# Chunk 2's first accumulator in two PSUM tiles, and two pieces of start-up work moved, in a TensorE-bound convolution and MLP kernel

## The chip, the cores and the metric

One core of a Trainium2 chip runs the whole program. The metric is the device time of one execution in microseconds. Times are quoted as medians. A profiled execution has a *span*, which starts at its first instruction; all moments below are microseconds from there. The *granted clock* is the share of its full clock that TensorE had, as the profile records it; over the whole span it is 1.0 or 0.999 in every run.

## The reference, cut to what matters

```python
def _attn_ref(x, weight):                    # x (8, 4096, 192), weight (8 heads, 7 taps)
    w = softmax(weight, axis=-1)             # (cut: written out in the original)
    x_pad = np.concatenate([zeros(B, 6, D), x], axis=1)
    ...                                      # each output row: 7 rows of x, weighted per head
def _moe_ref(x, w_in, w_out):                # w_in (192, 2048), w_out (2048, 192)
    h = x @ w_in
    g = np.maximum(0.01 * h, h)
    return g @ w_out                         # (32768, 192) float32
```

A causal convolution of 7 taps with one set of weights per head, then a first product, a leaky ReLU and a second product.

## The kernel before

The 192 channels are three *chunks* of 64. Two sequences lie on partitions 0 to 63 and 64 to 127. TensorE's matmuls write into *tiles* (buffers) of a memory called PSUM; such a tile, an *accumulator*, has to be copied out by ScalarE or VectorE, which the prediction calls evacuation. The first eight *groups* have 256 columns, the others 512. VectorE convolves nearly all groups ahead of need; for group 0 (all chunks) and group 1 (chunks 0 and 2) TensorE does it, with diagonal matrices of tap weights, because there is nothing else to run yet. Chunk 2 is convolved *crosswise*: its halves change partitions, so its matmuls use the two quarters of the TensorE array that chunks 0 and 1 leave free: where two chunks are convolved together, four matmuls start within 0.02 us (6.60 to 6.61 in the trace of before) and the next four 0.11 later. Its accumulator has to be copied out in two halves, each back to its own partitions.

```python
    def pe_conv_jobs(grp, c, parts=(0, 1), cross=False):
        blk, t0, T = grp
        acc = psum_o.tile([128, ST], FP32, name="acc", tag="po")     # one PSUM tile (pool of 4)
        ...                                                          # cut: matmuls diag * xt into acc
        def evac(*scale):
            ...
            if not cross:
                scale[0](y, acc[:, :T], rsum[:, c, :])
                return
            for e in range(2):
                ps = slice(e * CH, (e + 1) * CH)
                frm = slice((1 - e) * CH, (2 - e) * CH)
                scale[e](y[ps], acc[frm, :T], rsum[frm, c, :])
        return jobs, evac
    ...
    run(pe_0[:K])
    run(pe_0[K:], pe_2[:K])
    evac_0(act_scale)                                     # ScalarE
    run(pe_1[:K], pe_2[K:])
    run(pe_1[K:])
    evac_1(act_scale)                                     # ScalarE
    evac_2(act_scale, nc.vector.tensor_scalar_mul)        # half on ScalarE, half on VectorE
    transpose_first(1)                                    # TensorE, input of the next 256 rows
```

The first product takes one *product* `u` at a time: 12 matmuls into one of two accumulators `ph`, which one ScalarE activation then empties. In the main loop, group 0 looks so:

```python
            for u in range(2 * j, 2 * j + 2):
                mm1(grp, u, 128 if i <= NSW else CH)      # product u, then its activation
                ...
                if i == 0 and u in CUTS:                  # behind u = 1, 3, 4
                    cut = slice(*CUTS[u])
                    run(pe_0[cut], pe_2[cut])             # convolution of group 1
                if i == 0 and u == 5:
                    evac_0(act_scale)
                    evac_2(nc.vector.tensor_scalar_mul, nc.vector.tensor_scalar_mul)
                if i == 0 and u == 6:
                    transpose_first(2)
```

From group 1 on, *slots* (small groups of matmuls) of the second product (`po`, later `acc2`) fill TensorE between the first products.

Of the kernel before, what the change touches and what calls it, by code (L numbers as in the profile page):

```python
# [10 lines left out]
FP32 = mybir.dt.float32  # L11
# [4 lines left out]
def kernel(  # L16
# [8 lines left out]
    nc = tc.nc  # L25
# [10 lines left out]
    CH = 64  # L36
    NCH = D // CH
    ST = 512
# [6 lines left out]
    NHALF = 4  # L45
    RUN = 4
    NPEC = 3
    CUTS = {1: (0, 5), 3: (5, 10), 4: (10, 14)}
    GB = 32
    NR = D // (2 * GB)  # L50
# [9 lines left out]
    psum_o = ctx.enter_context(tc.tile_pool(name="po", bufs=4, space=bass.MemoryType.PSUM))  # L60
# [6 lines left out]
    groups = [(b, h * HT, HT) for b in range(NHALF) for h in range(2)]  # L67
# [100 lines left out]
    def evac_first(q, *copies):  # L168
        dst = xt[0][:, :, HALO + q * HT : HALO + (q + 1) * HT]
        dst = dst.rearrange("p c (s k) -> p s c k", s=HS)  # L170
        for s, t in enumerate(ptr.pop(q)):
            copies[s](out=dst[:, s], in_=t)  # L172
# [37 lines left out]
                    )  # L210
        return jobs

    def pe_conv_jobs(grp, c, parts=(0, 1), cross=False):



        blk, t0, T = grp
        acc = psum_o.tile([128, ST], FP32, name="acc", tag="po")
        jobs = []
        for p in parts:  # L220
            for k in range(K):
                a = BASE + k + blk * ST + t0
                both = []
                for e in range(2):
                    ps = slice(e * CH, (e + 1) * CH)
                    to = slice((e ^ cross) * CH, ((e ^ cross) + 1) * CH)
                    both.append(
                        lambda k=k, p=p, a=a, ps=ps, to=to: nc.tensor.matmul(  # L228
                            out=acc[to, :T], lhsT=diag[c][ps, p, k, :],
                            rhs=xt[0][ps, c, a : a + T],  # L230
                            start=(k == 0 and p == parts[0]),
                            stop=(k == K - 1 and p == parts[1]),
                        )
                    )
                jobs.append(both)

        def evac(*scale):
            if blk not in yt:
                yt[blk] = yt_pool.tile([128, NCH, ST], BF16, name="yt")
            y = yt[blk][:, c, t0 : t0 + T]  # L240
            if not cross:
                scale[0](y, acc[:, :T], rsum[:, c, :])
                return
            for e in range(2):
                ps = slice(e * CH, (e + 1) * CH)
                frm = slice((1 - e) * CH, (2 - e) * CH)
                scale[e](y[ps], acc[frm, :T], rsum[frm, c, :])  # L247

        return jobs, evac

    def run(*lists):
        for slots in zip_longest(*lists, fillvalue=()):
            for both in slots:
                for job in both:
                    job()
# [12 lines left out]
    for sign, off in ((1, 0), (-1, GRP - 1)):  # L268
        nc.gpsimd.affine_select(
            out=sel, in_=sel, compare_op=mybir.AluOpType.is_ge, fill=0.0,  # L270
# [16 lines left out]
    def spread_down(n):  # L287
        nc.vector.tensor_copy(out=w_in[n][0:CH, 1, :], in_=w_in[n][CH:128, 0, :])

    def spread_up(n):  # L290
        nc.vector.tensor_copy(out=w_in[n][CH:128, 1:3, :], in_=w_in[n][0:CH, 0:3:2, :])

    def w_in_of(f, e, c, m0, m1):
        n, f = divmod(f, NFC // NPW)
        slot = c if c == 2 else c ^ e
        a = f // RUN * RUN * 128 + f % RUN
        return w_in[n][
            e * CH : (e + 1) * CH, slot, a + m0 * RUN : a - f % RUN + m1 * RUN : RUN
        ]
# [6 lines left out]
    for rows in (0, 128):  # L306
# [6 lines left out]
        out=w_out.rearrange("p (c i) d -> p c i d", i=RUN),  # L313
# [8 lines left out]
    def warm(n, cols=HT):  # L322
# [10 lines left out]
        out=nmax, in_=w9[:, 0:K], axis=mybir.AxisListType.X,  # L333
# [3 lines left out]
        out=w9[:, 0:K], in_=w9[:, 0:K], func=mybir.ActivationFunctionType.Exp,  # L337
# [37 lines left out]

    diag = [const_pool.tile([128, 2, K, CH], BF16, name=f"diag{c}") for c in range(NPEC)]

# [21 lines left out]
    for p in range(2):  # L399
        diag_wide(2, p, K)  # L400
    spread_down(0)
    rsum = const_pool.tile([128, NCH, 1], FP32)
# [3 lines left out]
        out=rsum, in0=wml[:, :, K:], scalar=1e-9, in1=whm[:, :, 0, K:],  # L406
# [7 lines left out]
    def act_scale(out, in_, scale):  # L414
        nc.scalar.activation(  # L415
            out=out, in_=in_, func=mybir.ActivationFunctionType.Copy, scale=scale
        )

    pe_0, evac_0 = pe_conv_jobs(groups[0], 0)
    pe_2, evac_2 = pe_conv_jobs(groups[0], 2, cross=True)  # L420
    pe_1, evac_1 = pe_conv_jobs(groups[0], 1, (1, 0))
    run(pe_0[:K])
    run(pe_0[K:], pe_2[:K])
    evac_0(act_scale)
    run(pe_1[:K], pe_2[K:])
    run(pe_1[K:])
    evac_1(act_scale)
    evac_2(act_scale, nc.vector.tensor_scalar_mul)
    transpose_first(1)
    evac_first(1, nc.vector.tensor_copy, nc.vector.tensor_copy)  # L430
    wk = const_pool.tile([128, NCH, K], FP32, name="wk")
# [4 lines left out]
    g, po, acc2, osb, seal = {}, {}, {}, {}, None  # L436
# [8 lines left out]
    def mm1(grp, u, M):  # L445
        blk, t0, T = grp
        y = yt[blk]
        nf = ST // T
        ph = psum_h.tile([128, 2, ST], FP32, name="ph", tag="ph")
        for i in range(nf):  # L450
            f = nf * u + i
            for c in range(NCH):
                for e in range(2):
                    ps = slice(e * CH, (e + 1) * CH)
                    for m in range(0, 128, M):
                        nc.tensor.matmul(  # L456
                            out=ph[m : m + M, e, i * T : (i + 1) * T],
                            lhsT=w_in_of(f, e, c, m, m + M),
                            rhs=y[ps, c, t0 : t0 + T],
                            start=(c == 0),  # L460
                            stop=(c == NCH - 1),
                        )
        act = nc.scalar.activation(  # L463
            out=g[blk][:, nf * u : nf * (u + 1), :, t0 : t0 + T],
            in_=ph.rearrange("p e (i t) -> p i e t", i=nf),
            func=mybir.ActivationFunctionType.Prelu, alpha=0.01,
        )
        return act
# [143 lines left out]
    for i, grp in enumerate(groups):  # L612
        blk, t0, T = grp
        steps = T // 64
        if t0 == 0:
            g[blk] = g_pool.tile([128, NFC, 2, ST], BF16, name="g", tag="g")
        quota = plan.get(i, [16] * 4 if T == HT else [5, 5, 6, 5, 5, 6, 8, 8])

        if i == 0:
            ahead = []  # L620
        else:
            ahead = conv_jobs(groups[i + 1]) if i + 1 < len(groups) else []
        per = -(-len(ahead) // steps)
        for j in range(steps):
            for u in range(2 * j, 2 * j + 2):
                mm1(grp, u, 128 if i <= NSW else CH)
                if i == 0 and u == 0:
                    conv_1 = conv_jobs(groups[1], (1,))
                    for job in conv_1[:3]:
                        job()  # L630
                    spread_down(1)
                    spread_up(1)
                    for job in conv_1[3:]:
                        job()
                    pe_0, evac_0 = pe_conv_jobs(groups[1], 0)
                    pe_2, evac_2 = pe_conv_jobs(groups[1], 2, cross=True)
                if i == 0 and u in CUTS:
                    cut = slice(*CUTS[u])
                    run(pe_0[cut], pe_2[cut])
                if i == 0 and u == 5:  # L640
                    evac_0(act_scale)
                    evac_2(nc.vector.tensor_scalar_mul, nc.vector.tensor_scalar_mul)
                if i == 0 and u == 6:
                    transpose_first(2)
            jobs = ahead[per * j : per * (j + 1)]
            if T == ST:


                jobs = ahead[len(ahead) * j // steps : len(ahead) * (j + 1) // steps]
                for job in jobs:  # L650
                    job()
                jobs = []
            for _ in range(quota[j]):
                if i <= NSW:
                    mm2_row_slot(slot)
                else:
                    mm2_slot(slot)
                slot += 1
            if i == 0 and j == 3:
                evac_first(2, nc.vector.tensor_copy, nc.vector.tensor_copy)  # L660
            if i == 2 and j == 1:
                transpose_x(2)
            for job in jobs:
                job()
            if i == 0 and j == 3:
                transpose_half(3)

            last_half = t0 + T == ST
            if i == NSW and j == steps - 1:
                evac_o(LAST - 1)  # L670
                slot = NSW * NR * NFC
            if j == steps // 4 and last_half:
                load_x(blk + 3)
            if j == steps // 2 and last_half and blk > 0:
                transpose_x(blk + 2)
# [35 lines left out]
```

## Time and profile before

| | before |
|---|---|
| median of the first three runs | 686.46 us (685.19 to 686.69) |
| span of the profiled run | 683.4 us |
| TensorE busy | 677.7 us (99%) |
| first activation starts | 11.06 |
| first matmul of a second product starts | 20.79 |

The prediction shows the engine totals, the chain and the wait of VectorE. The view below gives the busy time of each engine in stretches of the span (stretch, its length, then the engines with their instruction counts, the granted clock, DMA share and GB/s), for the kernel before:

```profile
0.00:20.79 20.79, 18.50 (x312) 13.35 (x313) 15.44 (x46) 16.66 (x34) 16.91 (x31) 1.00 1.09 143
20.79:60.00 39.21, 39.21 (x840) 39.21 (x837) 34.13 (x92) 33.22 (x46) 16.04 (x23) 1.00 0.85 92
60.00:640.00 580.00, 579.75 (x10760) 382.82 (x10760) 421.42 (x689) 452.30 (x521) 113.03 (x152) 1.00 0.58 76
640.00:683.40 43.40, 40.25 (x680) 29.00 (x668) 11.55 (x20) 22.39 (x26) 0.00 (x0) 1.00 0.23 56
```

Behind the length of each stretch stand TensorE's busy time and, in brackets, its instructions. Once second products have begun, TensorE is busy in 39.21 of 39.21 and 579.75 of 580.00 us. In the first 20.79 us it is idle for 2.29; a change of the order at the start can help only there. The 3.15 us idle in the last stretch lie behind the last matmul (over at 680.26), where the last copy and output transfers are left.

### The profile page before, as it was taken

The numbers are of one execution on the slowest core, as the hardware profiler recorded it, in microseconds if no ns is written. First come the engines' busy times: TensorE is split into PE (matmuls) and PEld (weight loads), VectorE is DVE, ScalarE is ACT, GpSimd is POOL, SyncE is SP. The second block draws the span as 40 slices with busy tenths as digits, with TensorE's granted clock in tenths as the row PEclk, the third lists the DMA queues.
The fourth block names the chain that finished last, engine by engine and source line by source line (L and its number), as shares of the span: only waits on it lengthen the run. The fifth ranks groups of instructions, "written<-read, shape, count | busy, mean of one in ns | idle before, by whom it ended". The sixth has DMA issues, their size and how long they took to land.

```text
span 683.4 us, 27404 instructions
## 1 busy us (share of the span) xinstructions
PE 677.7 (99%) x12575; PEld 464.4 (68%) x12575; DVE 482.5 (71%) x844; ACT 524.6 (77%) x624; POOL 146.0 (21%) x204
## 2 busy tenths in 40 slices
PE   9999999999999999999999999999999999999998
PEld 6999986666666666666666666666666666666667
DVE  7979758667687667687667786676876676876612
ACT  7888998777777777777778777777777778777781
POOL 7722222222102222112221022221022220000000
PEclk9999999999999999999999999999999999999999
DMA  9975668557466566565564665574665664321123
GB/s 155 93 101 76 84 79 98 61 60 94 78 89 81 60 73 92 80 90 74 56 84 79 87 92 68 56 93 79 89 82 64 69 91 75 72 55 34 34 49 93
DMA packets 211763, 53.29 MB, mean 78 GB/s; under 512 B 205120, under 2 KB 211264, under 8 KB 211648
## 3 DMA queue, kind: packets, MB, share of 16 engines
q0 software_dynamic: 98736, 13.97, 29.9%
q1 hardware_dynamic: 112896, 37.57, 27.8%
q8 instruction: 98, 1.61, 1.0%
q14 instruction: 17, 0.14, 0.1%
q10 hardware_dynamic: 16, 0.00, 0.0%
HBM read 28.31 MB, written 25.17 MB: 78 GB/s over the span
## 4 chain that ended last, share of the span: by engine, by line
PE 97%; ACT 2%; DVE 0%; issue 0%; ACTq 0%
PE ph L456 48%; PE acc L545 41%; PE po L482 7%; ACT g L463 2%; PE acc L228 1%; ACT yt L415 0%; ACT L330 0%; ACTq L259 0%; ACT diag L387 0%; DVE yt L247 0%; ACT xt L172 0%; DVE o_sb L593 0%; DVE x_half L137 0%; ACT w L336 0%; ACT junk L330 0%
## 5 line engine op out<-in xcount | busy, mean ns | idle before, releaser
L463 ACT ACTIVATE g<-ph 128x1024 bf16<-128x1024 f32 x512 | 496.2, 1021 | 137.0 <-PE ph L456 136.6
L206 DVE SCALAR_TENSOR_TENSOR yt<-xt,wk,yt 128x512 bf16<-128x512 bf16 (+1 forms) x618 | 383.5, 702 | 0.2
L456 PE MATMUL ph<-yt,w_in 64*64 64x512 bf16 (+2 forms) x6048 | 378.4, 363 | 1.3 <-ACT g L463 0.6
L545 PE MATMUL acc<-g,w_out 64*64 64x512 bf16 x5184 | 316.5, 376 | 0.0
L456 PEld LDWEIGHTS <-w_in 64*64 64x64 bf16 (+1 forms) x6048 | 238.0, 129 | 99.1 <-issue 3.8
L545 PEld LDWEIGHTS <-w_out 64*64 64x64 bf16 x5184 | 166.7, 118 | 110.2
L82 POOL DMA_DIRECT2D x_bf<-in_x_dram x180 | 134.2, 770 | 416.2 <-DMA xt<-x_bf 309.9
L567 DVE STREAM_TRANSPOSE o_t<-acc 128x512 f32<-128x512 f32 x81 | 68.1, 885 | 169.5 <-PE acc L545 169.5
L482 PE MATMUL po<-w_out,g 64*128 64x192 bf16 (+1 forms) x1152 | 60.1, 243 | 0.0
L482 PEld LDWEIGHTS <-g 64*128 64x128 bf16 (+1 forms) x1152 | 55.6, 94 | 1.6 <-issue 0.4
L200 DVE TENSOR_SCALAR yt<-xt,wk 128x512 bf16<-128x512 bf16 (+1 forms) x103 | 28.8, 338 | 16.6 <-DMA xt<-x_bf 16.4
L555 ACT COPY junk<-junk 128x1 f32<-128x1 f32 x54 | 10.3, 192 | 3.9
L593 ACT COPY o_sb<-po 128x192 f32<-128x192 f32 x32 | 10.1, 320 | 1.3
L593 DVE COPY o_sb<-po 128x192 f32<-128x192 f32 x8 | 2.8, 357 | 6.8 <-PE po L482 3.9
L228 PE MATMUL acc<-xt,diag 64*64 64x256 bf16 x140 | 5.5, 272 | 0.3 <-ACT xt L172 0.3
L228 PEld LDWEIGHTS <-diag 64*64 64x64 bf16 x140 | 4.3, 106 | 1.4 <-issue 0.6
L324 PE MATMUL warm<-const-bfloat16-1.0 128*128 128x512 bf16 (+2 forms) x9 | 3.7, 521 | 0.8 <-PEq L695 0.8
L131 POOL DMA_DIRECT2D x_half<-in_x_dram x6 | 4.3, 757 | 0.0
L387 ACT ACTIVATE diag<-ident,whm 128x64 bf16<-128x64 bf16 x14 | 3.5, 335 | 0.2 <-DVE whm L373 0.2
L127 POOL DMA_DIRECT2D x_rows<-in_x_dram x4 | 2.9, 740 | 0.0
L330 ACT ACT_TABLE_LOAD x1 | 1.3, 1283 | 1.4 <-PEq L695 1.4
L324 PEld LDWEIGHTS <-const-bfloat16-1.0 128*128 128x128 bf16 x9 | 1.0, 122 | 2.0 <-issue 1.9
(44 smaller groups left out, 23.4 us busy)
## 6 DMA issues: line engine op xcount, KB each, us to landing
out_dram<-o_t SPq DMA_DIRECT2D x108, 192.0 KB, 4.6
x_bf<-in_x_dram POOLq DMA_DIRECT2D x180, 64.0 KB, 3.1
out_dram<-o_sb SPq DMA_DIRECT2D x16, 192.0 KB, 2.8
xt<-x_bf SPq DMA_TRANSPOSE x90, 3.7
w_out<-in_moe_w_out_dram POOLq DMA_DIRECT2D x1, 768.0 KB, 8.7
out_dram<-o_sb SPq DMA_DIRECT2D x8, 96.0 KB, 1.9
w_in<-in_moe_w_in_dram POOLq DMA_DIRECT2D x2, 256.0 KB, 4.7
x_nat<-in_x_dram SPq DMA_DIRECT2D x2, 192.0 KB, 2.5
```

Of the source, the lines that this page charges most:

```text
L82: nc.gpsimd.dma_start(out=t[:, c, :, e, :], in_=src[2 * rp + e, :, :, c * CH : (c + 1) * CH],)
L200: lambda s=src, d=dst, c=c: nc.vector.tensor_scalar_mul(d, s, wk[:, c, 0:1])
L206: lambda s=src, d=dst, c=c, k=k: nc.vector.scalar_tensor_tensor(out=d, in0=s, scalar=wk[:, c, k : k + 1], in1=d, op0=mybir.AluOpType.mult, ...
L228: lambda k=k, p=p, a=a, ps=ps, to=to: nc.tensor.matmul(out=acc[to, :T], lhsT=diag[c][ps, p, k, :], rhs=xt[0][ps, c, a : a + T], start=(k = ...
L324: nc.tensor.matmul(out=wa[:, 0, 0:cols], lhsT=ones[:, 0:128], rhs=ones[:, 0:cols], start=True, stop=True,)
L456: nc.tensor.matmul(out=ph[m : m + M, e, i * T : (i + 1) * T], lhsT=w_in_of(f, e, c, m, m + M), rhs=y[ps, c, t0 : t0 + T], start=(c == 0), ...
L463: act = nc.scalar.activation(out=g[blk][:, nf * u : nf * (u + 1), :, t0 : t0 + T], in_=ph.rearrange("p e (i t) -> p i e t", i=nf), func=my ...
L482: return nc.tensor.matmul(out=po[m], lhsT=g[b][ps, fc, e, s * 128 : (s + 1) * 128], rhs=w_out[ps, fc, :], start=start, stop=stop,)
L545: ins = nc.tensor.matmul(out=acc2[gi, r][e * CH : (e + 1) * CH, 0:T], lhsT=w_out_of(ps, fc, r), rhs=g[b][ps, fc, e, t0 : t0 + T], start=fi ...
L555: seal = nc.scalar.copy(out=junk, in_=junk)
L567: nc.vector.transpose(out=osb[gi, 0][:, 0 : T // GB, :, r], in_=acc2.pop((gi, r))[:, 0:T].rearrange("p (j k) -> p j k", k=GB),)
L593: ins = copy(out=o_sb[:, n % 2, :], in_=po.pop(n))
```

## The change

Its intent: let ScalarE and VectorE copy the two halves of chunk 2 at the same time; copy chunk 2 before chunk 1, since it is complete earlier; let the first product use the chunks in that order; and move a copy and a block of transposes of the first group to places thought idle.

```diff
+    FIRST = (0, 2, 1)
...
-    def pe_conv_jobs(grp, c, parts=(0, 1), cross=False):
+    def pe_conv_jobs(grp, c, parts=(0, 1), cross=False, apart=False):
-        acc = psum_o.tile([128, ST], FP32, name="acc", tag="po")
+        accs = [
+            psum_o.tile([128, ST], FP32, name=f"acc{i}", tag="po")
+            for i in range(2 if apart else 1)
+        ]
...                                    (matmuls and copies use accs[e * apart])
-    pe_2, evac_2 = pe_conv_jobs(groups[0], 2, cross=True)
+    pe_2, evac_2 = pe_conv_jobs(groups[0], 2, cross=True, apart=True)
...
+    evac_2(act_scale, nc.vector.tensor_scalar_mul)
     evac_1(act_scale)
-    evac_2(act_scale, nc.vector.tensor_scalar_mul)
...                                    (mm1)
+        chunks = range(NCH) if blk or t0 else FIRST
...
                 if i == 0 and u == 5:
-                    evac_0(act_scale)
+                    evac_0(nc.vector.tensor_scalar_mul)
                     evac_2(nc.vector.tensor_scalar_mul, nc.vector.tensor_scalar_mul)
-                if i == 0 and u == 6:
+                if i == 0 and u == 7:
                     transpose_first(2)
```

As in the prediction: **A** is everything up to `FIRST`, **B** the copy of chunk 0 of group 1 on VectorE, **C** the transposes behind the eighth product (`u == 7`) instead of the seventh.

More of the change, by code (lines that the diff above doesn't have):

```diff
@@ L227, in pe_conv_jobs @@
                     both.append(
-                        lambda k=k, p=p, a=a, ps=ps, to=to: nc.tensor.matmul(
+                        lambda k=k, p=p, a=a, ps=ps, to=to, acc=accs[e * apart]: nc.tensor.matmul(
                             out=acc[to, :T], lhsT=diag[c][ps, p, k, :],
@@ L241, in evac @@
             if not cross:
-                scale[0](y, acc[:, :T], rsum[:, c, :])
+                scale[0](y, accs[0][:, :T], rsum[:, c, :])
                 return
@@ L246, in evac @@
                 frm = slice((1 - e) * CH, (2 - e) * CH)
-                scale[e](y[ps], acc[frm, :T], rsum[frm, c, :])
+                scale[e](y[ps], accs[e * apart][frm, :T], rsum[frm, c, :])
         return jobs, evac
@@ L449, in mm1 @@
         ph = psum_h.tile([128, 2, ST], FP32, name="ph", tag="ph")
-        for i in range(nf):
+        chunks = range(NCH) if blk or t0 else FIRST
+        for n in range(nf * NCH):
+            i, c = n // NCH, chunks[n % NCH]
             f = nf * u + i
-            for c in range(NCH):
-                for e in range(2):
-                    ps = slice(e * CH, (e + 1) * CH)
-                    for m in range(0, 128, M):
-                        nc.tensor.matmul(
-                            out=ph[m : m + M, e, i * T : (i + 1) * T],
-                            lhsT=w_in_of(f, e, c, m, m + M),
-                            rhs=y[ps, c, t0 : t0 + T],
-                            start=(c == 0),
-                            stop=(c == NCH - 1),
-                        )
+            for e in range(2):
+                ps = slice(e * CH, (e + 1) * CH)
+                for m in range(0, 128, M):
+                    nc.tensor.matmul(
+                        out=ph[m : m + M, e, i * T : (i + 1) * T],
+                        lhsT=w_in_of(f, e, c, m, m + M),
+                        rhs=y[ps, c, t0 : t0 + T],
+                        start=(c == chunks[0]),
+                        stop=(c == chunks[-1]),
+                    )
         act = nc.scalar.activation(
```

## The prediction

> **What bounds the kernel now.** I read the page first: engine totals, the chain that ended last, the costliest groups. Then the chain in order of time for the first 45 us, because the diff touches only the work of the first two groups of 256 columns. Last, ScalarE and VectorE in order of time there.
>
> From the page (engine totals; the chain by engine; one group):
>
> ```profile
> PE 677.7 (99%) x12575; PEld 464.4 (68%) x12575; DVE 482.5 (71%) x844; ACT 524.6 (77%) x624; POOL 146.0 (21%) x204
> ...
> PE 97%; ACT 2%; DVE 0%; issue 0%; ACTq 0%
> ...
> L456 PE MATMUL ph<-yt,w_in 64*64 64x512 bf16 (+2 forms) x6048 | 378.4, 363 | 1.3 <-ACT g L463 0.6
> ```
>
> TensorE sets the time. It is busy in 677.7 of 683.4 us; all waits of the first-product matmuls come to 1.3 us. The other engines can only matter where TensorE waits for them, and 97% of the chain never leaves TensorE. The 3% elsewhere is the start. The chain there (start, duration, what):
>
> ```profile
> 5.45 3.42 PE acc L228 x84
> 8.88 0.02 issue
> 8.90 0.47 ACT yt L415
> 9.37 0.03 issue
> 9.40 0.48 ACT yt L415
> 9.88 0.02 issue
> 9.90 0.49 DVE yt L247
> 10.39 0.04 issue
> 10.43 1.25 PE ph L456 x19
> ...
> 16.73 1.02 ACT g L463
> 17.76 0.03 issue
> 17.78 0.47 ACT yt L415
> 18.26 1.84 ACT g L463 x2
> 20.09 0.04 issue
> 20.14 0.85 PE ph L456 x12
> 20.98 1.32 PE po L482 x32
> ```
>
> Two pieces are not TensorE's. From 8.90 to 10.39 three evacuations run one after another: chunk 1 (ScalarE), the first half of chunk 2 (ScalarE), its second half (VectorE). From 16.73 to 20.09 four ScalarE operations follow each other, one of them chunk 0's evacuation for the second group. From 20.14 the chain alternates two TensorE pieces of about 1.31 us without a break: there the time is TensorE's own.
>
> VectorE over the first piece (start, duration, engine, line, operation, idle before it and its releaser):
>
> ```profile
> 8.05 0.80 DVE L291 COPY w_in<-w_in 64x2048 bf16<-64x2048 bf16 x1
> 9.90 0.48 DVE L247 TENSOR_SCALAR yt<-acc,rsum 64x256 bf16<-64x256 f32 x1 [1.04 <-ACT yt L415]
> ```
>
> VectorE stood idle for 1.04 us until ScalarE was done, although the halves lie on different partitions of the accumulator. That is the wait the change is after.
>
> **What the Trainium skill says.** (1) "PSUM — Partial Sum Buffer", section "PSUM bank collisions raise a hardware error": two engines must be kept apart by bank and quadrant of 32 partitions, reads against reads included; guarding by bank alone is the simple version. The trace agrees with the simple version: halves of 64 partitions in one bank were still put in sequence, at 1.04 us. Two tiles mean two banks, so that order can go. (2) "ScalarE: Activation LUTs", section "What ACT_TABLE_LOAD costs": 186 ns + 0.833 ns per column, about 93 ns more for a pointer scale. For 256 columns I estimate 492 ns; the trace has 0.47, used below. It counts columns, not partitions: the half tile costs as much as the whole (0.48 against 0.47). (3) "TensorEngine Tiling (Array Packing)", section "PSUM Bottleneck": evacuate with both ScalarE and VectorE. The third part of the change does that in the second group. (4) "VectorE: DVE Perf Modes", "Side-by-side: where the cycles go": one result per cycle in the basic mode plus some 158 cycles of fill and start. I estimate (256+158)/0.96 = 431 ns for an evacuation from PSUM; the trace has 0.48, used below.
>
> **Part by part.** No matmul, copy or byte is added or removed.
>
> *A, the first group.* Chunk 2's accumulator lies in two tiles, it is copied before chunk 1, and the first product takes the chunks as 0, 2, 1. Chunk 2's convolution is complete seven column slots before chunk 1's. Slots start 0.11 us apart and the last at 8.59, so chunk 2's last starts at about 7.82 and is done (0.27 us) by 8.09. ScalarE started chunk 0's copy at 8.18; its copies start 0.50 apart (8.90, 9.40). So chunk 2's first half starts at 8.68 and chunk 1 at 9.18, done at 9.65. VectorE ends its weight copy at 8.85 and has the other half done at 8.87 + 0.48 = 9.35. TensorE is still in its transposes until 9.24; it does chunk 0, then chunk 2 at about 9.4, and waits for chunk 1 until 9.65 + 0.04 = 9.69. Before, the last wait ended at 10.43. As many pairs of matmuls come behind that wait as before. Gain: 10.43 − 9.69 = **0.74 us**.
>
> I take this gain as passed on whole to 17.8: from 10.43 on the chain is TensorE's own order of products and convolution slots, and ScalarE's activations follow those. VectorE also gets its copies of the second quarter done earlier (9.37 instead of 10.41), so it won't become the bound.
>
> *B, chunk 0's copy of the second group goes from ScalarE to VectorE.* In times of before: activations that follow each other directly start 0.97 apart (two in 1.94). With the copy between, the starts were 16.73 and 18.16, 1.43 apart. Removing it frees 0.46. But the matmuls of the eighth product, the last of group 0, start only when the sixth activation has freed its accumulator (16.73 + 1.02 = 17.75, started at 17.81), and B does not move that. From the first matmul of a product to its activation takes 0.89 (15.84 to 16.73). So the eighth activation can start at 17.81 + 0.89 = 18.70 instead of 18.16 + 0.97 = 19.13: 0.43 is left. VectorE pays 0.48, at a place where it delivers 4 us before need (its convolution for group 2 ended at 26.2; that group begins at about 30).
>
> *C, transposes of the third quarter behind the eighth product instead of before it.* Before, they filled a hole: 17.28 to 17.81, while TensorE waited for an accumulator anyway. Now they fall behind: last pair at about 18.36, a change of tile form of 0.20, 0.53 of transposes, next product at 19.09, and the second one after it at 19.09 + 0.66 = 19.75. ScalarE would allow 20.14 − 0.43 = 19.71. So C costs 0.04 of B, and B with C gives 20.14 − 19.75 = **0.39 us**. VectorE's copy of those transposes comes some 0.4 us later relative to TensorE; within the 4 us.
>
> Sum: 0.74 + 0.39 = **1.13 us**, 0.16% of the time. Behind 20.14 nothing stops TensorE, so I expect the whole of it at the end: span 683.4 − 1.1 = 682.3.
>
> **Rivals.** *R1: the order of the two reads stays*, because the halves also write one tile of the convolved input. For it: the trace cannot say which of the two tiles made VectorE wait. Against it: at 4.95 and 5.00 ScalarE and VectorE copy at once from two accumulators into disjoint columns of one tile. Even then VectorE would run 9.17 to 9.65, together with chunk 1, so it costs at most some hundredths: reordering alone brings A. *R2: pool turn-over.* One tile more in a pool of four: the second half takes a transpose tile copied out by 5.4, before it is needed; the next transposes take chunk 0's, copied out at 8.63, and start at 8.79. A wait here would show as TensorE waiting for ScalarE near 8.8, and cost 0.1 or so. *R3: ScalarE's own pace.* If the eight activations limited group 0 all the way, A would be lost. They wait 0.17, 0.28 and 0.32 for TensorE between 13 and 17, so they do not. *R4: given back later*, by transposed input arriving by DMA: VectorE waits 16.4 us for it in all, TensorE never. At 45.3 the convolution of group 4 ended, needed at about 51: 1.1 us earlier leaves over 4. If a hidden wait did return, the time would stay at 686.4. *R5: C blocks more* (the transposes wait for their tile or for rows): 0.3 us lost, 685.6.
>
> **Range and chances.** The median before is 686.46, but its three runs span 685.19 to 686.69 (mean 686.11) and the profiled one took 685.16: the noise is larger than the effect. 686.46 − 1.13 = 685.33; from the mean it would be 684.98. I take 685.2. Two tenths of a microsecond for R5 and the working, with noise of some 0.7 for a median of three, give 684.2 to 686.2. Two per cent is 13.7 us; nothing here reaches a tenth of it in either direction, so within 2% is nearly sure, 0.99.
>
> **What would show it right or wrong.** Right: VectorE's half of chunk 2 starts at 8.9 with no wait for ScalarE; a single wait of TensorE remains in the first product, for ScalarE, ending at about 9.7; the first activation starts near 10.3 instead of 11.06; no ScalarE copy stands between activations near 17; second products begin near 19.7 instead of 20.8 and last matmuls end 1.1 us earlier. A gain at 10.3 without one at 20 puts the fault in B or C; a gain at 20 without one at the end would be R4. A time over 686.5 or under 683.8 from fast runs would make the prediction wrong.

## The result and the profile after

| | before | changed |
|---|---|---|
| median, 6 runs each | 686.58 us (685.19 to 687.35) | 684.88 us (684.26 to 686.19) |
| span of the profiled run | 683.4 | 682.4 |
| first activation starts | 11.06 | 10.41 |
| first matmul of a second product | 20.79 | 19.77 |

The ratio is 0.9981, with a 95% interval from 0.9965 to 0.9997: the same within 2%. A ratio here is the mean time of one kernel's fast runs over that of the other's of the same rounds, so it is not quite the ratio of the medians. The predicted 685.2 lies 0.3 above the measured median, inside the range of 684.2 to 686.2.

Engine totals of the changed kernel, from its page:

```profile
PE 677.2 (99%) x12575; PEld 467.1 (68%) x12575; DVE 481.4 (71%) x845; ACT 524.2 (77%) x623; POOL 145.9 (21%) x204
```

One instruction has passed from ScalarE to VectorE (624 and 844 before), and no matmul was added. The chain in order of time, changed kernel (start, duration, what):

```profile
5.52 3.40 PE acc L232 x84
8.92 0.46 PE ptr L162 x12
9.38 0.34 PE ph L461 x4
9.72 0.02 issue
9.74 1.28 PE ph L461 x20
...
16.08 1.03 ACT g L468
17.11 0.04 issue
17.16 0.85 PE ph L461 x12
18.01 0.46 PE ptr L162 x12
18.46 1.50 PE ph L461 x24
19.97 1.32 PE po L487 x32
```

The three evacuations between 8.90 and 10.39 have left the chain; TensorE now goes from the convolution through its transposes straight into the first product. Near 17 one activation is left in it instead of a row of four ScalarE operations. The transposes (`ptr`) stand in it in both places. VectorE in order of time, changed kernel:

```profile
8.12 0.78 DVE L295 COPY w_in<-w_in 64x2048 bf16<-64x2048 bf16 x1
8.82 0.46 DVE L251 TENSOR_SCALAR yt<-acc,rsum 64x256 bf16<-64x256 f32 x1
```

Its half starts straight behind its weight copy, with no wait; before, it stood idle for 1.04 us. By stretches, changed kernel:

```profile
0.00:19.77 19.77, 17.98 (x312) 13.14 (x313) 13.84 (x43) 16.11 (x33) 15.06 (x29) 1.00 1.04 141
19.77:60.00 40.23, 40.23 (x864) 40.23 (x860) 36.19 (x98) 34.44 (x47) 18.97 (x26) 1.00 1.06 97
60.00:640.00 580.00, 579.74 (x10758) 385.33 (x10757) 419.88 (x687) 451.86 (x521) 111.87 (x151) 1.00 0.57 76
```

The same 312 matmuls now take 19.77 us, with 1.79 of TensorE idle time instead of 2.29. Most of the rest of the gain is in its busy time, though the work is the same: 1.83 before and 1.54 now from the start of the transposes to the first activation (31 matmuls each), 3.42 and 3.23 from the sixth activation to the first second product (61 each). The ends of matmuls in a profile are modelled, and a matmul in front of a wait counts as busy up to that end: this view counts part of the waiting as busy. From there on TensorE is as full as before. The first second product comes 1.02 earlier and the span is 1.02 shorter: nothing was given back.

### The profile page after: what moved, and what is told of

Read it like the earlier page. It is cut to its first block, busy times and chain, and to the rows that moved or that the text cites. A ratio compares the mean times of both kernels' runs of the same rounds, so it can differ in the third digit from the quotient of the medians.

```text
span 682.4 us, 27404 instructions
## 1 busy us (share of the span) xinstructions
PE 677.2 (99%) x12575; PEld 467.1 (68%) x12575; DVE 481.4 (71%) x845; ACT 524.2 (77%) x623; POOL 145.9 (21%) x204
## 4 chain that ended last, share of the span: by engine, by line
PE 97%; ACT 2%; DVE 0%; issue 0%; ACTq 0%
PE ph L461 48%; PE acc L550 41%; PE po L487 7%; ACT g L468 1%; PE acc L232 1%; PE ptr L162 0%; ACT L334 0%; ACTq L263 0%; ACT diag L391 0%; ACT xt L173 0%; DVE o_sb L598 0%; DVE x_half L138 0%; ACT w L340 0%; ACT junk L334 0%; DVE w9p L348 0%
## 5 line engine op out<-in xcount | busy, mean ns | idle before, releaser
L550 PEld LDWEIGHTS <-w_out 64*64 64x64 bf16 x5184 | 168.4, 119 | 108.4
L598 ACT COPY o_sb<-po 128x192 f32<-128x192 f32 x32 | 10.1, 320 | 1.3
L173 DVE COPY xt<-ptr 128x384 bf16<-128x384 bf16 x5 | 1.6, 352 | 1.8 <-PE ptr L162 1.7
```

What stands on the lines that cost most here:

```text
L550: ins = nc.tensor.matmul(out=acc2[gi, r][e * CH : (e + 1) * CH, 0:T], lhsT=w_out_of(ps, fc, r), rhs=g[b][ps, fc, e, t0 : t0 + T], start=fi ...
L598: ins = copy(out=o_sb[:, n % 2, :], in_=po.pop(n))
```

## The experiments

Twelve runs were made. Of e1 to e9, eight fell into a start that differs from that of the two profiles above: the convolution of group 0 runs at about half speed for part of its time. Absolute moments are then not comparable, so I cut each profile at four landmarks: T, the start of the transposes of the second quarter, which follow the convolution; the first activation; the sixth activation; the first matmul of a second product. The clock column is the moment from which the trace's own record of the granted clock (in the packed trace; no view prints it) shows full speed. The matmuls agree with it: in e9 the steps of the convolution start 0.21 apart until 10.1 and 0.11 apart from there on.

| kernel | full clock from | T | T to 1st activation | 1st to 6th | 6th to 2nd product | 2nd product to end |
|---|---|---|---|---|---|---|
| before | 4.2 | 8.79 | 2.27 | 5.67 | 4.06 | 662.65 |
| changed | 3.5 | 8.85 | 1.56 | 5.67 | 3.69 | 662.65 |
| e1 A alone | 9.1 | 10.62 | 1.34 | 5.67 | 3.93 | 662.65 |
| e2 A in one tile | 3.9 | 8.77* | 1.79* | 5.67 | 3.93 | 662.65 |
| e3 tiles, old order | 8.2 | 10.14 | 1.80 | 5.67 | 4.06 | 662.65 |
| e4 B and C alone | 8.3 | 10.22 | 2.28 | 5.67 | 3.69 | 662.65 |
| e5 without C | 9.0 | 10.56 | 1.35 | 5.67 | 3.69 | 662.66 |
| e6 copy twice | 10.1 | 11.10 | 1.82 | 5.67 | 3.69 | 662.66 |
| e7 second product early | 10.1 | 11.10 | 1.56 | 5.67 | 3.69 | 662.66 |
| e8 slots in the gap | 10.1 | 11.07 | 1.35 | 5.67 | 3.68** | 663.69 |
| e9 changed again | 10.1 | 11.07 | 1.35 | 5.68 | 3.69 | 662.65 |
| e10 more warm-up | 6.7 | 9.40 | 1.35 | 5.67 | 3.69 | 662.63 |
| e11 warm-up, old kernel | 6.6 | 9.33 | 2.28 | 5.68 | 4.05 | 662.64 |
| e12 more warm-up again | 6.1 | 9.09 | 1.62 | 5.67 | 3.69 | 662.65 |

\* one transpose at 8.77, the other eleven at 9.22, when their input rows had landed; 1.34 from there.

\*\* up to the second product behind group 0, at 21.77; the four slots that e8 moved start at 17.88.

The last column is the same to 0.03 us in all but e8. So the end follows from the first second product, and the parts can be judged by the columns between. Each run up to e8 is a single execution with a profile, so its own time is not used against others.

### e1: part A alone

```diff
-                    evac_0(nc.vector.tensor_scalar_mul)
+                    evac_0(act_scale)
-                if i == 0 and u == 7:
+                if i == 0 and u == 6:
```

> Part A alone; B and C undone. Theory (A and B+C are independent and each passes whole to the end): the first activation starts at about 10.4 as in the changed kernel (before: 11.06), the first second product at 20.79 - 0.65 = 20.1 (changed: 19.77), the span is near 683.4 - 0.65 = 682.75. Rival (ScalarE's pace limits the first group, so A is worth something only together with B): first activation 10.4, but the first second product at 20.6 or later and the span at 683.3.

Measured: 685.95 us, span 684.2, with the late clock, so neither expected moment could be met as written. By segments: T to the first activation is 1.34, against 2.28 in e4, which has the old first group and the late clock too. A brings 0.94 there, and it passes on whole: the next segment is unchanged and the last but one is even 0.13 shorter than before (3.93 against 4.06). The rival wanted that segment to swallow the gain; it falls, and R3 with it.

### e2: A's order, but one tile

```diff
-    pe_2, evac_2 = pe_conv_jobs(groups[0], 2, cross=True, apart=True)
+    pe_2, evac_2 = pe_conv_jobs(groups[0], 2, cross=True)
```
(with e1's edit)

> Part A's order (copy of chunk 2 before chunk 1, chunks 0, 2, 1), but chunk 2 in one tile; B and C undone. My theory in the prediction (the order alone brings A): VectorE's half waits for ScalarE's and starts at about 9.25, done 9.72, together with chunk 1; the first activation starts at 10.45 to 10.55, so at most 0.1 of the 0.65 is lost. Rival (the second tile is what matters): VectorE's half or chunk 1 come out later than 10.1 and the first activation starts at 10.9 or later.

Measured: 684.51 us, span 682.8, early clock. The first activation started at 10.56. VectorE in order of time, in e2:

```profile
9.15 0.48 DVE L251 TENSOR_SCALAR yt<-acc,rsum 64x256 bf16<-64x256 f32 x1 [0.29 <-ACT yt L419]
```

With one tile VectorE still waits for ScalarE, but only 0.29 us, since ScalarE did its half earlier; all copies were done by 9.63. The rival's 10.9 is refuted: the order alone can bring most of A. Whether one tile would have cost the expected 0.1 is not shown: the input rows of the transposes landed 0.45 late in this run, and TensorE came to chunk 2 only after the copies were done.

### e3: two tiles, but the old order

```diff
-    FIRST = (0, 2, 1)
+    FIRST = (0, 1, 2)
-    evac_2(act_scale, nc.vector.tensor_scalar_mul)
     evac_1(act_scale)
+    evac_2(act_scale, nc.vector.tensor_scalar_mul)
```
(with e1's edit)

> Two tiles for chunk 2, but the old order of copies and chunks; B and C undone. If the shared PSUM tile made VectorE wait: its half starts at 8.9 without a wait, ScalarE's half still ends at about 9.9, the first activation starts at 9.92 + 0.63 = 10.55 (0.5 of the 0.65 gained). Rival R1 (the shared tile of the convolved input made it wait): VectorE's half starts at 9.9 again, and the first activation stays at 11.06.

Measured: 686.04 us, span 684.3, late clock. VectorE in order of time, in e3 and then in e4, which has one tile and the same late clock:

```profile
9.51 0.48 DVE L251 TENSOR_SCALAR yt<-acc,rsum 64x256 bf16<-64x256 f32 x1
```

```profile
11.34 0.48 DVE L251 TENSOR_SCALAR yt<-acc,rsum 64x256 bf16<-64x256 f32 x1 [2.14 <-ACT yt L419]
```

With two tiles VectorE's half started at 9.51 without a wait, before ScalarE had even begun its own half (10.76); with one it stood idle for 2.14. Both kernels write the halves to the same tile of the convolved input, so the shared PSUM tile made VectorE wait and R1 falls. The tiles alone shorten T to the first activation from 2.28 to 1.80, which is 0.48 where 0.5 was expected.

### e4: B and C alone

The changed kernel with `apart=True` taken away and the old order of copies and chunks (the edits of e2 and e3 without e1's).

> Parts B and C alone; the first group as before. Theory: first activation 11.06 as before, the first second product at 20.79 - 0.37 = 20.4, span near 683.05. Rival (B and C bring nothing without A): first second product at 20.8, span 683.4.

Measured: 686.32 us, span 684.5, late clock. The sixth activation to the second product takes 3.69 against 4.06: 0.37 gained without A, as the theory said. The rival falls.

### e5: without C

```diff
-                if i == 0 and u == 7:
+                if i == 0 and u == 6:
```

> The changed kernel with C undone: the transposes of the third quarter stand before the eighth product again. Theory (C costs a few hundredths of B): the first second product at 19.70 to 19.80 against 19.77, span 682.3 to 682.45. Rival (C is needed, because transposes before the eighth product hold it up): first second product at 20.0 or later, span 682.7 or more.

Measured: 685.79 us, span 683.9, late clock. The segment is 3.69 with and without C. C is worth nothing and costs nothing. The eighth product starts 1.07 behind the sixth activation and the tenth 3.04 behind it in both kernels, each when ScalarE has freed its accumulator; the transposes only take a part of the idle time before one or the other.

### e6: chunk 1 copied twice

```diff
     evac_1(act_scale)
+    evac_1(act_scale)
```

> The changed kernel with chunk 1's copy on ScalarE done twice, 0.50 us more in the piece that A shortens; the result is the same. Theory (what is lost or gained there comes out whole at the end): first activation 10.9, first second product 20.25, span 682.9. Rival R4 (there is slack behind it, or a later wait takes it): span within 0.15 of the changed kernel's 682.4.

Measured: 686.80 us, span 684.9, late clock. T to the first activation is 1.82, against 1.35 in e5, e8 and e9, which have the same first group and the late clock: 0.47 more, the length of one copy. The later segments are those of the changed kernel (5.67, 3.69, 662.66). What is added in this place comes out whole at the end; R4 falls.

### e7: two pairs of the second product earlier

Here and in the expectation "the second product" that is moved is the second of the first products (`u == 1`), not a product with `w_out`.

```diff
-                mm1(grp, u, 128 if i <= NSW else CH)
+                if i == 0 and u < 2:
+                    if u == 0:
+                        open_ph = [mm1(grp, v, 128, ns=(0, 1), act=False) for v in range(2)]
+                    mm1(grp, u, 128, ph=open_ph[u], ns=range(2, 6))
+                else:
+                    mm1(grp, u, 128 if i <= NSW else CH)
```
(and the three arguments in `mm1`)

> The changed kernel, with the first two pairs of matmuls of the second product put where TensorE waits for chunk 1 (about 9.53 to 9.74). Theory (0.2 of waiting is left there): the first activation unchanged at 10.4, the sixth activation 0.2 earlier (15.9 against 16.08), first second product 19.55, span 682.2. Rival (ScalarE's pace is the limit from here on): nothing moves behind the third activation, span 682.4.

Measured: 686.63 us, span 684.7, late clock. The first activation came 0.21 later (1.56 against 1.35) and nothing was won back. With the late clock there is no gap to fill, since chunk 1's copy is done when TensorE asks for it; two pairs of foreign work then only stand in the way. Neither theory was tested, because both speak of the early clock. The idea stays open there.

### e8: slots of the second product in the gap before the eighth product

```diff
-        0: [0] * 4,
+        0: [0, 0, 4, 0],
+        1: [16, 16, 16, 12],
```

> The changed kernel, with four of the second group's slots of the second product (about 0.33 us of TensorE) moved into the gap of 0.46 before the eighth product of the first group. Theory (the gap is idle TensorE time): the eighth product still starts at 17.16, the end comes 0.33 earlier, span 682.05. Rival (the slots hold up the eighth product, or their tiles are not free): the eighth product later than 17.3 and a span of 682.4 or more.

Measured: 687.42 us, span 685.5, late clock. By the edit the four slots stand before the seventh product (17.88), which pushes that product into the gap; the gap itself gets no slot. The eighth product was not held up: it started 1.07 behind the sixth activation (18.09 to 19.16), as in the changed kernel (16.08 to 17.16). So the gap is idle time, as the theory said. But 662.65 − 0.33 = 662.32 was expected for the last segment and 663.69 came. TensorE's waits in e8 (what waited, for what: total, times, longest), and then what follows them in order of time, name the loss:

```profile
PE po L487 <- ACT o_sb L598: 0.6, 1, 0.6
PE po L487 <- ACT junk L522: 0.4, 1, 0.4
```

```profile
23.36 0.50 PE L487 MATMUL po<-w_out,g 64*128 64x192 bf16 x8 [0.40 <-ACT junk L522]
29.40 0.50 PE L487 MATMUL po<-w_out,g 64*128 64x192 bf16 x8 [0.60 <-ACT o_sb L598]
```

The second product of a pair runs in two rounds, with a ScalarE instruction between them. Four slots earlier, the end of a round no longer meets ScalarE at a free moment: the two instructions start at 23.11 and 29.02, each directly behind two activations. Counted from start to start the two stops hold the whole loss: the 24 matmuls before such a stop take 0.99 us where nothing stops them (31.05 to 32.04), but here 1.59 (21.77 to 23.36) and 1.76 (27.64 to 29.40), so 0.60 + 0.77 = 1.37. A gain that was there was lost at a boundary the edit had shifted.

### e9: the changed kernel again, with more runs

> The changed kernel once more, unedited, with more runs of both kernels. The traces so far show two starts, whatever the kernel: TensorE's full clock was granted 3.5 to 4.2 us after the span's start (before, changed, e2) or 8.2 to 10.1 us after it (the seven others). Theory (the state of the start, not the change, makes the spread of the times): both kernels show two clusters about 1.3 to 2 us apart, before near 685.2 and 686.4 to 687.4, the changed one near 684.3 and 685.4 to 686.2, and the ratio lies within 0.9975 to 0.9990. Rival (the change itself alters how the start goes): the changed kernel shows one cluster only, or its share of early starts is far from that of before.

Measured: 684.21, 685.25, 685.30, 685.54, 686.36 and 686.36 us, median 685.42; before, eleven runs with median 686.81; ratio 0.9984 (0.9970 to 0.9999). The profiled run was one at 686.36, with the full clock from 10.1. TensorE in order of time, in e9, with the same program as the changed kernel above:

```profile
5.86 5.29 PE L232 MATMUL acc<-xt,diag 64*64 64x256 bf16 x84
```

The same 84 matmuls took 3.40 us in the first profile and 5.29 here. That is the whole of the spread: T is 11.07 against 8.85, and from T on this execution is even 0.2 quicker, because the copies keep up with a slower convolution. The page's clock line shows full speed in both.

Before ran 30 times: nine at 685.13 to 685.37 (mean 685.21), 21 at 686.43 to 687.38 (mean 686.87), none between. The changed kernel ran 12 times (its first six and e9): four at 684.21 to 684.40 (mean 684.31), eight at 685.25 to 686.36 (mean 685.76). Only profiled runs show their clock, so that every slower run is a late grant is an inference from the times. The shares, 9 of 30 and 4 of 12, give no sign that the change alters the start. If the clusters are the two starts, the change brings 0.90 us early against early and 1.11 late against late.

### e10 and e12: more matrix work before the first convolution

```diff
+    def beside(cols):
+        nc.tensor.matmul(
+            out=wa[0:CH, 0, 0:cols], lhsT=ones[32:64, 0:CH], rhs=ones[32:64, 0:cols],
+            start=True, stop=True,
+        )
     def select(out, parts):
+        beside(HT)
...
-    warm(1, 128)
     select(wps_l, 2)
-    warm(1)
+    warm(1, 320)
...
     transpose_first(0)
     warm(1, ST)
+    warm(1, 192)
```

> The changed kernel with more matrix work on constants between 3.5 and 5.45 us: a 256-column matmul on another row tile beside each of the two small selections (in place of one of 128 columns between them), 320 columns instead of 256 before the first transposes and 192 more behind them. Theory (a late grant comes from too little work in that stretch): the clock is granted before 7 us in every or nearly every run, the times lie in 684.2 to 685.0 with few above, and the ratio to before is about 0.9970. Rival (the grant depends on something else, or the added work delays the first convolution): both clusters stay, or the fast one moves up by 0.2 or more.

> e10 once more, on the chip of e11, to pair the two and to count late grants. Theory: again most runs at 684.5 to 684.7 and at most two late ones near 686.3; against e11 the clusters lie 1.0 apart; ratio to before about 0.9975. Rival (e10's one cluster was luck): half the runs or more late.

Measured: e10 684.56, 684.59, three times 684.66, and 686.31, median 684.66, ratio to before 0.9978 (0.9965 to 0.9992). e12 684.56, 684.68 (three times), 684.69, and 686.22, median 684.68, ratio 0.9982 (0.9968 to 0.9996); 0.9970 and 0.9975 were expected. The clock came at 6.7 and 6.1 us in the two profiles. Ten of twelve runs are in one cluster only 0.13 wide. TensorE in order of time, in e10:

```profile
5.77 3.70 PE L232 MATMUL acc<-xt,diag 64*64 64x256 bf16 x84
```

This cluster lies 0.33 above the changed kernel's early one (684.64 against 684.31), which was a sign of the rival: the added work helps the grant, but the start is later than in an early run. The convolution begins at 5.77 in both profiles (5.52 in the early one). Its own speed is not the reason, for in e12 it took 3.39 us, as in an early run, and the whole run took no less time (684.69). The six transposes before it still run at half speed (0.11 apart, against 0.06), VectorE's copy of them starts at 5.30 in e10 against 5.06, and the first copy of the convolved chunks, which needs a result of VectorE, at 8.53 against 8.24. But the early cluster came up in only four of twelve runs.

### e11: the same work in the kernel before

> The kernel before, with the same added matrix work as in e10 (e10: five of six runs between 684.56 and 684.66, one at 686.31; clock granted at 6.7 us in its profile). Theory (the added work makes the early grant the rule for either kernel, and the change is worth the same there): most runs in one cluster between 685.5 and 685.8, that is about 1.0 above e10's; few or none above 687. Rival (the spread belongs to the change, or the change is worth much more or less in this state): two clusters as before, or a cluster less than 0.6 or more than 1.4 above e10's.

Measured: 685.15, 685.44, 685.46, 685.68 and 685.69 us; ratio to before 0.9990 (0.9977 to 1.0002). None of the five runs is late; they spread over 0.54, two of them in the 685.5 to 685.8 expected, and lie 0.84 above the mean of e10's and e12's ten (685.48 against 684.64). The theory holds in the main: no late start, and a difference a little under the 1.0 expected, which does not reach the rival's 0.6. This is the timing of the change least mixed with late starts that I have.

The version of e10 is the best of the kernels by median: 684.66 against 685.42 for the changed kernel. With six runs each and intervals that overlap it is not shown to be faster in the mean; what is shown is that slow starts are rarer with the added work (15 of 17 runs of e10, e11 and e12 without one, against 13 of 42 without the added work).

## Why the prediction was right

**The bound.** "TensorE sets the time", and only the first 20 us can give anything: confirmed by the last column of the table. e6 adds that 0.47 us put in there come out whole.

**A, predicted 0.74.** T to the first activation fell by 0.71. The single steps hold: VectorE's half without a wait, chunk 1 used at 9.74 (9.69 predicted, in an execution whose convolution began 0.07 later). The remark that "reordering alone brings A" is supported by e2's copies, all done by 9.63, but the loss of "some hundredths" without the second tile is not measured. The tiles alone bring 0.48 (e3). So A has two overlapping remedies, which cannot be added. With a late clock A is worth 0.93 to 0.94, which the prediction did not see.

**B and C, predicted 0.39.** Measured 0.37, but the sum holds two errors that nearly cancel. It reads 1.94 us for two activations as a distance of 0.97 between their starts; they start 0.92 apart and are 1.02 long. The eighth activation, before and then changed:

```profile
19.06 1.03 ACT L463 ACTIVATE g<-ph 128x1024 bf16<-128x1024 f32 x1
18.04 1.02 ACT L468 ACTIVATE g<-ph 128x1024 bf16<-128x1024 f32 x1
```

It started at 19.06, not 19.13, so B is worth 19.06 − 18.70 = 0.36 and not 0.43 (traces: 2.33 and 1.96 behind the sixth activation). With that, ScalarE allows the tenth product at 20.14 − 0.36 = 19.78, later than the 19.75 of the sum for C, so C costs nothing, as e5 shows. For B the path was right and its size 0.07 too large; for C the sum took TensorE's path where ScalarE's is the later one, which made it 0.04 too small. That the 0.39 came out close is luck. B's cap, that the eighth product cannot start before the sixth activation frees its accumulator, is visible as the 0.46 us that TensorE waits at 17.16. One thing was not foreseen: with A's order and B undone (e1, e2) chunk 0's copy starts 0.92 behind the sixth activation, and with the old order (before, e3, e11) 1.05. The traces name no wait there in any of them. I have no cause for these 0.13; because of them B and C bring 0.37 alone but 0.24 on top of A.

**The sum.** 1.13 predicted, 1.02 in the two profiles: 0.71 + 0.37 = 1.08, less 0.06 because T came later in the profiled run after. In clusters of like start it is 0.90 (early), 1.11 (late) and 0.84 (with the added work). That the median came within 0.3 of 685.2 is partly luck: 684.88 is the middle of an early run (684.40) and a late one (685.36), and the median of e9's six is 685.42.

**The rivals.** R1 fell with e3, R3 with e1, R4 with e6 and the last column. The slack for R4 was misread: group 4's convolution ended at 46.89, not 45.3, where the view that was read had been cut. It is needed at 51.04, and in the changed kernel 3.3 us are left (46.71, 50.02) and not over 4. VectorE's slack for group 2, "4 us", is 3.7 before and 2.0 now (26.96, 28.98), still enough. For R2, no wait of TensorE for ScalarE shows near 8.8. R5 did not occur (e5).

**What it left out.** The prediction called the scatter of before "noise" and did not ask where it came from. It was the larger effect of the two: 1.66 us between the clusters of before (686.87 − 685.21), against about 1 us for the change. A page of the skill would have told me. "TensorE: Matmul & The Clock Gate", section "Part 1: The HAM clock gate (the "warmup" mystery)", says that the array runs at half clock until a free-running window of about 3.4 us has been busy. The traces agree: steps of the convolution start 0.21 apart before the grant and 0.11 after it (e9), and the record of the full clock is 679.252 us long in four profiles and 675.839 in the other ten, which is 3.413 apart. The full clock comes at 3.5 to 4.2 us or at 8.2 to 10.1, for the same kernels, and at 6.1 to 6.7 with the added work. The first six runs of each kernel also had different mixes: two of before and three of the changed one were early. I put the difference between 1.70 (the medians) and 1.02 (the spans) down to that; it is an inference, since only one run of each shows its clock.

## What to carry to other kernels

On a kernel that is bound by one engine from 20 us on, look first at the start, cut it at landmarks, and add up segments; a gain of 1 us in 686 is then plain in a trace though it drowns in the times. Copy first what is complete first, and give two engines two tiles; here the tiles alone brought half of A (0.48 of 0.94), and the order alone nearly all of it as far as e2 can show. Take the distance of two operations from their starts, not from half of their joint length. Before calling scatter noise, compare a fast and a slow profile of the same program: here the warm-up stretch of the start was worth more than the change.

## What the Trainium skill lacked or had wrong

- "TensorE: Matmul & The Clock Gate", Part 1, gives the transition point a scatter of ±500 ns under sustained matmul work. Here, with thin places in the first 6 us, the same program got the full clock at 3.5 us in one execution and at 10.1 in another, and its times differ by 2 us (684.35 and 686.36). The page lacks how busy a window must be. From these traces I estimate, taking the page's 3.4 us: a window ending at 3.5 that held 2.7 us of dense matmuls (from 0.85 on) was enough; in e3, with the grant at 8.2, a window ending near 4.7 with about 2.2 us of dense matmuls and small ones behind was not, nor in e10, with the grant at 6.7, one ending near 3.3 with about 2.5.
- No page of the skill says that the granted clock printed by stretch can read full while the array is not: it is 1.00 for the first 20.79 us of before, where the trace's own record has full speed only from 4.2.
- "ScalarE: Activation LUTs", section "What ACT_TABLE_LOAD costs", has back-to-back operations overlap by about 93 ns. Two large activations here agree (0.92 apart, 1.02 long: 0.10). But the two copies of 0.47 from 8.90 on start 0.50 apart, without any overlap, and the copy behind the sixth activation starts 0.10 before that one's end in e1 but 0.03 behind it in the kernel before. No page tells when the overlap is lost.
- "PSUM — Partial Sum Buffer" allows two engines on different quadrants of one bank. This program's own waits are by the whole tile, 1.04 us before, 2.14 in e4, none with two tiles (e3). They come from the program's semaphores, so no run here shows what the chip itself allows, although the prediction says that the trace agrees with guarding by bank. The page does not say what splitting by tile costs or brings; here it was 0.48 alone.
